# Bias attention and gated feed-forward: one queue for the loads and bias stores, and a float32 path for the first eight units

## The chip, the cores and the metric

One core of one Trainium2 chip. The metric is device time in microseconds (us) of one execution; several runs give a median, and one execution is profiled.

## What is computed

Cut to what matters (B=4, H=8, S=576, D=64; DM=512, DFF=2048):

```python
scores = q @ k.T / 8 + bias            # bias[h,i,j] = (relu(log1p(|i-j|)/log1p(max(i,1)) * w1 + b1)) @ w2
attn   = exp(scores - rowmax); attn = attn / (rowsum + 1e-9)
x      = (attn @ v) as [B*S, H*D]      # 2304 x 512
h      = x @ w_in                      # 2304 x 2048
out    = (h * sigmoid(1.702 * h)) @ w_out
```

The bias does not depend on the batch. All inputs are float32 (the weights of the feed-forward part are float64, and are loaded as pairs of 32-bit words and merged to float32).

## The kernel before, in words

**Precision.** Most products run in float16 with each operand split into a high and a low half, so one product is three float16 matmuls (high·high, high·low, low·high). The split of an operand costs a high half (a scaled copy, mostly on ACT) and a low half (`lo_part`, line 464, on DVE).

**Attention units.** There are 72 units: a query chunk c (four of 128 rows, a last one of 64), a pair of heads hp, a batch b. The first eight are all of chunk 0, batches 0 and 1. A unit runs `scores` (L601, TensorE); `reduce` (L609, DVE: adds the bias, finds the row extreme); `expo` (L618, ACT, with row sums); `inverse` (L625, L627); `exp_hi` (L639 on ACT, or L635 on DVE) and `exp_lo` (L464); `turn` (L649), a DMA transpose on SyncE's queue, which needs 16-bit data; `av` (L662, 30 float16 matmuls of 128 columns); `x_split` (L679 and L464, both on DVE), which writes the unit's part of x.

**Bias.** For each chunk c there are eight groups (four in the last chunk): four `relu` on DVE or ACT by the letters of BIAS_ENG (L382, L380), `products` (L397, float32 matmuls of 32-column weights), `bias_evict` (L400, ACT), `bias_store` (L406, a DMA to scratch memory in HBM from ACT's queue). A unit's `bias_load` (L448, SyncE's queue) waits for all stores of its chunk.

**Weights.** 32 pieces. Each is a load (L738), three merging operations on DVE (L745, L749, L753), a high half on ACT (L767), a low half on DVE (L464 into `wi` or `wo`).

**Feed-forward part.** Ten blocks of 256 rows (two of 128, blocks 4 and 9), each with 16 steps f: `m1` (L796), `tanh` (L803, ACT), `gate_mul` (L809, DVE), `gate_hi` (ACT for the blocks in ACT_G, else DVE; L817, L819), `gate_lo` (DVE for the blocks in VEC_G, else GpSimd; L824), `m2` (L833). Block 0 needs all eight first units and, by its end, all 32 weight pieces.

**Order.** Nothing is scheduled by hand. `Plan.order` is a list scheduler that runs while the kernel is built: every task has an engine, an assumed duration, dependencies, buffers taken and given back, and a priority, here a due time (`U_AT` for units, `W_AT` for weights, `B1_AT` and `B2_AT` for bias groups, leads for K, Q and V loads). The engine's instructions come out in the order the plan starts them, and each engine then executes strictly in that order: an instruction that waits holds up all behind it on its engine or queue. The plan treats at most eight DMAs of SyncE's and ACT's queues as outstanding at a time (the "hw" lanes). SLACK is added to each assumed DMA end; `hold` makes SyncE's queue busy in the plan until shortly before a transfer's assumed end.

**Queues.** Loads of q and k, 26 of the weights, V of batches 2 and 3, the bias loads and all transposes go through SyncE's queue; V of batches 0 and 1 and the first six weight pieces through GpSimd's; bias and output stores through ACT's.

```python
W_POOL = 6
(nc.gpsimd if i < W_POOL else nc.sync).dma_start(...)     # load_w
queue = nc.gpsimd if b < 2 else nc.sync                   # load_v
nc.scalar.dma_start(out=scr[c]..., in_=slot(("os", c, s))...)   # bias_store
```

Of the kernel before, what the change touches and what calls it, by code (L numbers as in the profile page):

```python
# [22 lines left out]
SLACK = 2000  # L23
# [3 lines left out]
class Plan:  # L27
# [6 lines left out]
    def add(self, eng, occ, fn, deps=(), after=(), take=(), give=(), prio=0.0, dma=0, lat=None, gate=-1, n_dma=1, mode=0, hold=False):  # L34
# [23 lines left out]
    def order(self):  # L58
# [7 lines left out]
        mode = 0  # L66
# [18 lines left out]
        while True:  # L85
            for e in ENGINES:
                while idle.get(e, 1e18) <= now and ready[e]:
# [34 lines left out]
                    if go["dma"]:  # L122
# [5 lines left out]
                        if go["hold"]:  # L128
                            occ = max(occ, end - 2000 - now)
# [34 lines left out]
def kernel(  # L164
# [45 lines left out]
    CAPS = {"ht": 6, "w64": 4, "w": 3, "kv": 3, "a32": 2, "hl": 2, "aT": 4, "bt": 3, "kT": 6, "os": 6, "qT": 3, "q": 2,  # L210
            "kt": 2, "ob": 2}
    LEAST = {"wide": {"kT": 1, "a32": 1, "hl": 1, "aT": 1, "bt": 1, "ht": 2, "w64": 1, "kv": 1},
             "narrow": {"w": 1, "os": 3, "qT": 2, "q": 1, "kt": 1, "ob": 1}}
    BIAS_ENG = ['VVVA', 'VVVA', 'VVVA', 'VVVA', 'VVVA', 'VVVA', 'VVVA', 'VVVA', 'AAAA', 'AAAA', 'AAAA', 'AAAA', 'AAAA', 'AAAA', 'VAAA', 'AAAA', 'AAAA', 'VAAA', 'AAAA', 'AAAA', 'AAAA', 'AAAA', 'AAAA', 'AAAA', 'AAAA', 'VVAA', 'VVAA', 'VVAA', 'VVAA', 'VVAA', 'VVAA', 'VVAA', 'VVVV', 'VAAA', 'VAAA', 'VVAA']
    VEC_EXP = {60: 2, 51: 1, 52: 1}
    ACT_G = {0, 3, 7}
    VEC_G = {1, 2, 7}
# [6 lines left out]
    Q_FROM, K_FROM, V_FROM = 6, 6, 4  # L224
    AV_FIRST, X_FIRST = 18.7, 6.2
# [24 lines left out]
    wi16 = cst.tile([128, 2, 4, DFF], F16, name="wi16")  # L250
    wo16 = cst.tile([128, NF, 2, DM], F16, name="wo16")
# [152 lines left out]

    def bias_store(c, s):
# [54 lines left out]
    qT_task, kT_task, v_task = {}, {}, {}  # L460
# [85 lines left out]
    def load_v(b, e):  # L546

        queue = nc.gpsimd if b < 2 else nc.sync
# [3 lines left out]
        queue.dma_start(  # L552
# [3 lines left out]
        queue.dma_start(out=t[0:64, :, 4, :], in_=va[:, SM:S, :].rearrange("u p d -> p u d"))  # L556
        queue.dma_start(
# [3 lines left out]
        queue.dma_start(  # L561
# [3 lines left out]
        queue.dma_start(out=t[64:128, :, 8, :], in_=vb[:, SM:S, :].rearrange("u p d -> p u d"))  # L565
# [370 lines left out]
```

## Time and profile before

| | |
|---|---|
| median of 3 runs | 690.97 us (690.25 to 692.12) |
| the profiled execution | 691.4 us, its span 689.6 us |
| mean granted TensorE clock | 0.954 |
| busy: PE, DVE, ACT, POOL | 617.3, 511.0, 427.8, 95.8 us (90%, 74%, 62%, 14%) |
| chain that ended last, by engine | PE 53%, DVE 21%, DMA 11%, ACT 8%, issue 4% |

PE is TensorE, DVE VectorE, ACT ScalarE, POOL GpSimd, SP SyncE; "q" behind an engine's name is its DMA queue. A busy share is an average over the span, and the stages of this kernel differ: it is read by stretches below. A row "line engine op out<-in shape xcount | busy, mean ns | idle before" is a group of equal instructions.

### The profile page before, as it was taken

The numbers are of one execution on the slowest core, as the hardware profiler recorded it, in microseconds if no ns is written. First come the engines' busy times: TensorE is split into PE (matmuls) and PEld (weight loads), VectorE is DVE, ScalarE is ACT, GpSimd is POOL, SyncE is SP. The second block draws the span as 40 slices with busy tenths as digits, with TensorE's granted clock in tenths as the row PEclk, the third lists the DMA queues.
The fourth block names the chain that finished last, engine by engine and source line by source line (L and its number), as shares of the span: only waits on it lengthen the run. The fifth ranks groups of instructions, "written<-read, shape, count | busy, mean of one in ns | idle before, by whom it ended". The sixth has DMA issues, their size and how long they took to land.

```text
span 689.6 us, 17456 instructions
## 1 busy us (share of the span) xinstructions
PE 617.3 (90%) x6888; PEld 383.7 (56%) x6888; DVE 511.0 (74%) x1432; ACT 427.8 (62%) x882; POOL 95.8 (14%) x157
## 2 busy tenths in 40 slices
PE   2766474799999998999889999999999999999997
PEld 1213242556565565656566666666666666666664
DVE  5579889999978887976877788889879884233232
ACT  2699897699967685664666766656746663222121
POOL 5210100111210000000011122111121111002222
PEclk9696875899999999999999999999999999999999
DMA  9999988998768559669998579979877763000000
GB/s 244 224 290 230 279 175 209 286 272 229 157 162 204 121 114 236 121 159 218 226 191 188 121 170 174 191 165 196 187 154 155 147 121 85 1 1 32 1 31 16
DMA packets 228082, 111.79 MB, mean 162 GB/s; under 512 B 209440, under 2 KB 211616, under 8 KB 228000
## 3 DMA queue, kind: packets, MB, share of 16 engines
q1 hardware_dynamic: 218224, 89.74, 61.4%
q10 hardware_dynamic: 7952, 15.43, 6.4%
q0 software_dynamic: 1824, 5.51, 2.6%
q8 instruction: 54, 0.88, 0.5%
q14 instruction: 28, 0.23, 0.1%
HBM read 52.85 MB, written 15.34 MB: 99 GB/s over the span
## 4 chain that ended last, share of the span: by engine, by line
PE 53%; DVE 21%; DMA 11%; ACT 8%; issue 4%; SPq 1%; POOL 0%; ACTq 0%; DVEq 0%; POOLq 0%
PE op L833 19%; PE hp L796 18%; DVE wide L464 6%; PE hp L662 6%; PE sp L601 5%; DVE wide L609 5%; DMA wide<-wide 3%; DMA wide<-in_k_dram 3%; DMA wide<-scr 2%; PE sp L397 2%; ACT wide L618 2%; ACT wide L639 2%; DVE th L809 2%; DVE narrow L749 2%; DVE narrow L753 1%
## 5 line engine op out<-in xcount | busy, mean ns | idle before, releaser
L796 PE MATMUL hp<-xT,wi 128*128 128x256 f16 (+1 forms) x1920 | 206.8, 262 | 2.6 <-DVE th L809 2.2
L833 PE MATMUL op<-wo,gT 128*128 128x512 f16 x864 | 205.2, 380 | 0.9 <-POOL gT L824 0.6
L796 PEld LDWEIGHTS <-wi 128*128 128x128 f16 x1920 | 170.3, 98 | 39.1 <-issue 10.4
L618 ACT ACTIVATE wide<-wide,sm 128x576 f32<-128x576 f32 x144 | 110.6, 769 | 93.1 <-DVE sm L609 92.7
L824 POOL TENSOR_TENSOR gT<-th,gT 128x256 f16<-128x256 f32 (+1 forms) x112 | 76.1, 681 | 536.3 <-ACT gT L817 302.0
L833 PEld LDWEIGHTS <-gT 128*128 128x128 f16 x864 | 77.8, 98 | 91.3 <-issue 5.5
L464 DVE SCALAR_TENSOR_TENSOR wide<-wide,sm,wide 128x576 f16<-128x576 f32 x144 | 119.4, 843 | 12.3 <-ACT wide L639 11.9
L803 ACT ACTIVATE th<-hp 128x256 f32<-128x256 f32 (+1 forms) x160 | 56.7, 355 | 100.6 <-PE hp L796 91.0
L809 DVE SCALAR_TENSOR_TENSOR th<-th,hp 128x256 f32<-128x256 f32 (+1 forms) x160 | 62.3, 390 | 72.4 <-ACT th L803 71.7
L609 DVE CUSTOM_DVE_ANT_0 wide<-sp,wide 128x576 f32<-128x576 f32 x144 | 105.3, 750 | 10.9 <-DMA wide<-scr 5.4
L639 ACT ACTIVATE wide<-wide,sm 128x576 f16<-128x576 f32 x140 | 103.8, 766 | 5.5 <-issue 3.0
L601 PE MATMUL sp<-wide,narrow 64*128 64x512 f16 (+1 forms) x960 | 69.5, 295 | 16.7 <-DVE wide L464 7.5
L662 PEld LDWEIGHTS <-v 128*64 128x64 f16 x2400 | 67.4, 114 | 26.6 <-issue 23.2
L662 PE MATMUL hp<-wide,v 128*64 128x128 f16 (+1 forms) x2190 | 67.1, 215 | 4.9 <-DMA wide<-wide 4.8
L380 ACT ACTIVATE wide<-tab,bp 128x576 f32<-128x576 f32 x96 | 69.3, 767 | 2.8 <-ACT narrow L400 1.6
L601 PEld LDWEIGHTS <-narrow 64*128 64x128 f16 (+1 forms) x960 | 29.5, 99 | 50.4 <-issue 30.1
L397 PE MATMUL op<-wide,pk 128*32 128x512 f32 (+1 forms) x224 | 34.1, 546 | 11.8 <-ACT wide L380 5.7
L625 DVE TENSOR_SCALAR sm<-sm 128x1 f32<-128x1 f32 x144 | 21.5, 149 | 21.2 <-ACT wide L618 20.4
L819 DVE CAST gT<-th 128x256 f16<-128x256 f32 (+1 forms) x112 | 30.8, 275 | 6.4 <-PE op L833 0.2
L397 PE MATMUL sp<-wide,pk 128*32 128x512 f32 (+1 forms) x352 | 29.4, 456 | 2.2 <-DVE sm L609 1.9
L397 PEld LDWEIGHTS op<-wide,pk 128*32 128x32 f32 x224 | 10.3, 130 | 35.2 <-ACT wide L380 14.4
L679 DVE TENSOR_SCALAR xT<-hp 128x128 f16<-128x128 f32 x72 | 20.4, 283 | 12.2 <-PE hp L662 11.9
(63 smaller groups left out, 451.5 us busy)
## 6 DMA issues: line engine op xcount, KB each, us to landing
wide<-scr SPq DMA_DIRECT2D x32, 576.0 KB, 5.3
scr<-narrow ACTq DMA_DIRECT2D x33, 288.0 KB, 3.5
wide<-in_moe_w_out_dram SPq DMA_DIRECT2D x14, 512.0 KB, 5.1
wide<-in_moe_w_in_dram SPq DMA_DIRECT2D x12, 512.0 KB, 5.5
wide<-in_k_dram SPq DMA_DIRECT2D x16, 256.0 KB, 5.3
narrow<-in_q_dram SPq DMA_DIRECT2D x16, 256.0 KB, 5.0
out_dram<-narrow ACTq DMA_DIRECT2D x16, 256.0 KB, 3.4
wide<-scr SPq DMA_DIRECT2D x8, 288.0 KB, 5.2
```

The source lines that it names most:

```text
L380: nc.scalar.activation(out=h, in_=tv, func=ACTF.Relu, bias=bp[:, pb:pb + 1])
L397: nc.tensor.matmul(to[32 * r:32 * r + 32], lhsT=w2b, rhs=rhs, start=True, stop=True)
L464: nc.vector.scalar_tensor_tensor(out=out, in0=in0, scalar=scale, in1=in1, op0=ALU.mult, op1=ALU.subtract)
L601: nc.tensor.matmul(pair[64 * e:64 * e + m, a, cs], lhsT=qt[r, x, hp + e, 0:m], rhs=kt[r, hp % 2 + e, y, cs], start=i == 0, stop=i == 2,)
L609: nc.vector.tensor_tensor_reduce(out=slot(("a32", u))[:, cs], in0=slot(("sp", u)).rearrange("p (h a) n -> p h (a n)", h=2)[:, a, 0:S], in1 ...
L618: nc.scalar.activation(out=t, in_=t, func=ACTF.Exp, scale=-1.0, bias=sm[:, a:a + 1], accum_out=sm[:, 2 + a:3 + a])
L639: nc.scalar.activation(out=hl_of(u)[:, 0, cs], in_=slot(("a32", u))[:, cs], func=ACTF.Identity, scale=r)
L662: nc.tensor.matmul(o[64 * a:64 * a + 64, po], lhsT=vt[:, x, vc:vc + 64], rhs=t[:, 9 * y + k0, po], start=kb < 0 and i == 0, stop=kb == 3 a ...
L796: nc.tensor.matmul(p[:, :n], lhsT=wi16[:, z, cc, 128 * f:128 * f + 128], rhs=r, start=i == 0, stop=i == 11,)
L809: nc.vector.scalar_tensor_tensor(out=th, in0=th, scalar=1.0, in1=slot(("hp", j, f))[:, :n], op0=ALU.add, op1=ALU.mult)
L824: (nc.vector if j in VEC_G else nc.gpsimd).tensor_tensor(out=gt[:, 1, :n], in0=th, in1=gt[:, 0, :n], op=ALU.subtract)
L833: nc.tensor.matmul(o[:, i], lhsT=gt[:, z, ts], rhs=wo16[:, f, y, :], start=f == 0 and n3 == 0, stop=f == NF - 1 and n3 == 2,)
```

## The change

All loads and the bias stores are issued on SyncE's queue. The first eight units (DIRECT = 8) no longer split their exponentials: DVE builds a diagonal matrix of the reciprocal row sums, TensorE multiplies the float32 exponentials by it, which transposes and scales them into PSUM, ACT or DVE copies that to SBUF, and `av_direct` multiplies in float32 with the unsplit values V. For these units `exp_hi`, `exp_lo`, the DMA transpose and the float16 `av` are gone. Beside this the first half of `x_split` goes to ACT for 11 units, 52 `exp_hi` are put on DVE outside the first eight units (4 before), 65 `relu` are on DVE (48 before; by chunk 24, 1, 7, 24, 9 where it was 24, 1, 1, 14, 8), blocks 0, 2, 3, 5, 6, 8, 9 have `gate_hi` on ACT (0, 3, 7 before), blocks 4 to 7 `gate_lo` on DVE (1, 2, 7 before), and the due times, leads, SLACK and buffer limits change. The weight buffers are laid out anew (`wi16`, `wo16` in one tile). A second way to hand over the first bias chunk (`bias_place`, `bias_keep`) is written down but PLACE is False, so it is not built.

```diff
-SLACK = 2000
+SLACK = 3000
...
-                            occ = max(occ, end - 2000 - now)
+                            occ = max(occ, end - go["hold"] - now)
...
-    CAPS = {"ht": 6, "w64": 4, "w": 3, "kv": 3, "a32": 2, "hl": 2, "aT": 4, "bt": 3, "kT": 6, "os": 6, "qT": 3, "q": 2,
+    CAPS = {"ht": 6, "w64": 4, "w": 3, "kv": 6, "a32": 3, "hl": 2, "aT": 4, "bt": 3, "kT": 6, "os": 6, "qT": 3, "q": 2, "dg": 2,
...
-    U_AT = (41.8, 8, 104.8, 8.89)
-    W_POOL = 6
-    W_AT = (19.7, 3, 5, 51.6, 1.95)
-    B1_AT = (10.5, 4.18)
-    B2_AT = (10.3, 6)
-    BT_LEAD, K_LEAD, Q_LEAD, V_LEAD, LOAD_LEAD, W_LEAD = -0.4, 5, 5, 6.5, 12, 12.2
+    DIRECT = 8
+    TURN_OUT = ['AAV', 'AAV', 'VAA', 'VAA', 'AAV', 'VAA', 'VVV', 'VVA']
+    X_ACT = {1, 2, 4, 6, 7, 8, 10, 12, 13, 14, 15}
+    V_LATE = {(0, 0): -21.9, (1, 0): 18.2, (0, 1): 138.3, (1, 1): 123.3}
+    U_AT = (17.5, 9.67, 92.1, 8.12)
+    W_FREE = 5
+    PLACE = False
+    W_AT = (1.0, 6.75, 9, 50.7, 5.81)
+    B1_AT = (6.1, 3.56)
+    B2_AT = (-6.7, 8.24)
+    BT_LEAD, K_LEAD, Q_LEAD, V_LEAD, LOAD_LEAD, W_LEAD = -5.9, 16.7, -4.2, 43.9, 4.3, -7.7
...
     def bias_store(c, s):
-        nc.scalar.dma_start(
+        nc.sync.dma_start(
...
-            scr_done[c].append(add("ACT", 20, lambda c=c, s=s: bias_store(c, s), [ev], give=[("os", c, s)],
+            scr_done[c].append(add("SP", 350, lambda c=c, s=s: bias_store(c, s), [ev], give=[("os", c, s)],
...
-        queue = nc.gpsimd if b < 2 else nc.sync
-        queue.dma_start(
+        nc.sync.dma_start(
...
+    def diagonal(u, a):
+        nc.vector.tensor_scalar(
+            out=slot(("dg", u))[:, 128 * a:128 * a + 128], in0=idn, scalar1=small[u % 8][:, 2 + a:3 + a], scalar2=None,
+            op0=ALU.mult,
+        )
+
+    def turn_pe(u, a):
+        t, d = slot(("a32", u)), slot(("dg", u))[:, 128 * a:128 * a + 128]
+        o, h = slot(("pt", u))[:, a], slot(("pt2", u))
+        nc.tensor.matmul(
+            h[64 * a:64 * a + 64, 0:128], lhsT=t[:, 512 + 64 * a:576 + 64 * a], rhs=d, start=True, stop=True,
+        )
+        for kb in range(4):
+            x = 640 * a + 128 * kb
+            nc.tensor.matmul(o[:, 128 * kb:128 * kb + 128], lhsT=t[:, x:x + 128], rhs=d, start=True, stop=True)
+
+    def turn_out(u, a):
+        t = slot(("aT", u))[:, 640 * a:640 * a + 512]
+        if TURN_OUT[u][a] == "A":
+            nc.scalar.copy(t, slot(("pt", u))[:, a])
+        else:
+            nc.vector.tensor_copy(t, slot(("pt", u))[:, a])
...
+        for kb in range(-1, 4):
+            for a in range(2):
+                po = slice(64 * a, 64 * a + 64) if kb < 0 else slice(0, 128)
+                k0 = 4 if kb < 0 else 5 * a + kb
+                nc.tensor.matmul(
+                    o[64 * a:64 * a + 64, 0:128], lhsT=vd[po, k0], rhs=t[po, k0],
+                    start=kb < 0, stop=kb == 3, skip_group_check=True,
+                )
...
+        if z == 0 and u in X_ACT:
+            nc.scalar.activation(out=d[:, 0], in_=o[:, 0:128], func=ACTF.Copy, scale=xs)
...
-        (nc.gpsimd if i < W_POOL else nc.sync).dma_start(out=slot(("w64", i))[:, 0:1024].bitcast(U32), in_=src)
+        nc.sync.dma_start(out=slot(("w64", i))[:, 0:1024].bitcast(U32), in_=src)
```

`turn_tail`, not shown, copies the last 64 key columns of both heads (128 x 128) from PSUM.

## Rows read from the trace of the kernel before

**Rows 1.** Busy time by stretch; columns: stretch, its length, five engines, clock, DMA, GB/s.

```profile
0.00:60.00 60.00, 32.38 (x232) 12.53 (x232) 38.60 (x87) 39.58 (x66) 16.45 (x40) 0.83 0.89 252
60.00:140.00 80.00, 52.80 (x575) 29.80 (x579) 74.12 (x183) 66.25 (x122) 5.84 (x8) 0.74 0.95 239
140.00:200.00 60.00, 58.90 (x640) 35.35 (x633) 55.62 (x138) 54.72 (x108) 10.90 (x13) 1.00 0.85 214
200.00:600.00 400.00, 388.75 (x4784) 248.82 (x4783) 316.62 (x948) 248.05 (x537) 45.02 (x64) 1.00 0.76 158
650.00:690.00 40.00, 34.48 (x322) 23.33 (x320) 11.88 (x42) 7.87 (x24) 10.82 (x22) 0.97 0.07 21
```

**Rows 2.** The chain that ended last, 0 to 130 us: start, length, what.

```profile
2.67 15.60 DMA wide<-in_k_dram
...
36.27 6.67 DMA scr<-narrow
43.21 7.71 DMA wide<-scr
```

**Rows 3.** DVE's groups by line and form, 0 to 60 us, with idle time before them.

```profile
L464 DVE SCALAR_TENSOR_TENSOR wide<-sp,wide 128x1152 f16<-128x1152 f32 x2 | 2.7, 1358 | 5.9 <-ACT wide L536 5.9
L357 DVE COPY ips<-hp 128x36 f32<-128x36 f32 x1 | 0.2, 196 | 6.7 <-ACT tab L339 6.7
```

**Rows 4.** DVE's groups by line and form, 0 to 200 us.

```profile
L464 DVE SCALAR_TENSOR_TENSOR wide<-wide,sm,wide 128x576 f16<-128x576 f32 x32 | 26.1, 825 | 0.0
...
L753 DVE SCALAR_TENSOR_TENSOR narrow<-wide,narrow 128x512 uint32<-128x512 uint32 x32 | 22.7, 711 | 0.1
L749 DVE SCALAR_TENSOR_TENSOR narrow<-wide,narrow 128x512 uint32<-128x512 uint32 x32 | 22.0, 687 | 0.1
L382 DVE TENSOR_SCALAR wide<-tab,bp 128x576 f32<-128x576 f32 x30 | 14.1, 525 | 1.7 <-PE op L397 1.6
L745 DVE TENSOR_SCALAR narrow<-wide 128x512 uint32<-128x512 uint32 x32 | 13.7, 429 | 0.0
L464 DVE SCALAR_TENSOR_TENSOR wi<-narrow,wi 128x512 f16<-128x512 f32 x16 | 11.0, 687 | 1.0 <-ACT wi L767 0.9
L464 DVE SCALAR_TENSOR_TENSOR wo<-narrow,wo 128x512 f16<-128x512 f32 x16 | 10.9, 684 | 3.6 <-ACT wo L767 3.5
L809 DVE SCALAR_TENSOR_TENSOR th<-th,hp 128x256 f32<-128x256 f32 x16 | 6.6, 414 | 0.7 <-ACT th L803 0.7
...
L679 DVE TENSOR_SCALAR xT<-hp 128x128 f16<-128x128 f32 x16 | 4.5, 282 | 3.0 <-PE hp L662 3.0
```

**Rows 5.** DVE's and ACT's groups by line and form, whole span.

```profile
L639 ACT ACTIVATE wide<-wide,sm 128x576 f16<-128x576 f32 x140 | 103.8, 766 | 5.5 <-issue 3.0 <-DVE sm L627 1.8 <-ACT wi L767 0.2
...
L819 DVE CAST gT<-th 128x256 f16<-128x256 f32 x80 | 23.1, 289 | 3.9 <-PE op L833 0.2
...
L635 DVE TENSOR_SCALAR wide<-wide,sm 128x576 f16<-128x576 f32 x4 | 2.0, 512 | 0.0
```

**Rows 6.** PE in order of time: start, length, instructions in a run.

```profile
16.21 1.08 PE L524 MATMUL sp<-idn,wide 128*128 128x128 f32 x4 [4.54 <-DMA wide<-in_k_dram]
...
88.59 1.81 PE L662 MATMUL hp<-wo,v 128*64 128x128 f16 x30
...
96.02 0.66 PE L524 MATMUL sp<-idn,wide 128*128 128x128 f32 x4 [0.28 <-DVE sm L609]
```

**Rows 7.** PE's groups by form, 84.7 to 86.3 us, clock low.

```profile
L601 PE MATMUL sp<-wide,narrow 64*128 64x512 f16 x6 | 1.6, 606 | 6.0 <-DVE wide L464 6.0
L397 PE MATMUL op<-wide,pk 128*32 128x512 f32 x2 | 1.1, 1060 | 0.0
```

**Rows 8.** DMA issues 30 to 60 us: queue, count, KB each, us from issue to landing.

```profile
wide<-scr SPq DMA_DIRECT2D x3, 576.0 KB, 10.1
scr<-narrow ACTq DMA_DIRECT2D x4, 288.0 KB, 5.4
...
wide<-in_moe_w_in_dram SPq DMA_DIRECT2D x2, 512.0 KB, 11.6
```

More of the change, by code (lines that the diff above doesn't have):

```diff
@@ L32, in __init__, with add @@
         self.env, self.refs = {}, {}
-    def add(self, eng, occ, fn, deps=(), after=(), take=(), give=(), prio=0.0, dma=0, lat=None, gate=-1, n_dma=1, mode=0, hold=False):
+    def add(self, eng, occ, fn, deps=(), after=(), take=(), give=(), prio=0.0, dma=0, lat=None, gate=-1, n_dma=1, mode=0, hold=0):
         t = dict(eng=eng, occ=occ, fn=fn, deps=list(deps), after=list(after), take=list(take), give=[], prio=prio,
@@ L410 @@
     t_near = [t_sd, t_sa, t_iv]
+    placed = []
     t_far = None
@@ L451 @@
         bk = (c, hp, b // 2)
-        if bk not in bt_task:
+        if (u >= 8 or not PLACE) and bk not in bt_task:
             bt_key[bk] = ("bt", u)
@@ L643, in exp_lo, with turn_tail, av_direct @@
         lo_part(hl_of(u)[:, 1, cs], slot(("a32", u))[:, cs], r, hl_of(u)[:, 0, cs])
+    def diagonal(u, a):
[18 more added lines that the diff above has]
+            nc.vector.tensor_copy(t, slot(("pt", u))[:, a])
+    def turn_tail(u):
+        t, o = slot(("aT", u))[:, 512:640], slot(("pt2", u))[:, 0:128]
+        nc.scalar.copy(t, o) if TURN_OUT[u][2] == "A" else nc.vector.tensor_copy(t, o)
+    def av_direct(u):
+        b, c, hp = units[u]
+        t = slot(("aT", u)).rearrange("p (c n) -> p c n", c=9)
+        o = slot(("ot", u))
+        vd = slot(("v32", b, hp // 2)).rearrange("p (u c d) -> p u c d", u=2, c=9)[:, hp % 2]
+        for kb in range(-1, 4):
[5 more added lines that the diff above has]
+                    start=kb < 0, stop=kb == 3, skip_group_check=True,
+                )
     def aT_of(u):
@@ L705 @@
         for a in range(2):
-            t = add("DVE", 676, lambda u=u, a=a: reduce(u, a), [st, bt_task[bk]],
+            t = add("DVE", 676, lambda u=u, a=a: reduce(u, a), [st] + (placed if PLACE and u < 8 else [bt_task[bk]]),
                     take=[("wide", "a32", ("a32", u))] if a == 0 else [], after=[t] if a else [],
-                    give=([("sp", u)] + ([bt_key[bk]])) if a else [], prio=p + 0.1 + 0.01 * a, lat=160)
+                    give=([("sp", u)] + ([] if PLACE and u < 8 else [bt_key[bk]])) if a else [], prio=p + 0.1 + 0.01 * a, lat=160)
+            if PLACE and u < 8:
+                first_use.append(t)
             ex = add("ACT", 757, lambda u=u, a=a: expo(u, a), [t], prio=p + 0.2 + 0.01 * a)
@@ L712 @@
                 iv = add("DVE", 65, lambda u=u, a=a, part=part: inverse(u, a, part), [iv], prio=p - 900)
+            if u < DIRECT:
+                dg = add("DVE", dve(128, ptr=1, fast=True), lambda u=u, a=a: diagonal(u, a), [iv], prio=p - 800,
+                         take=[("narrow", "dg", ("dg", u))])
+                tp = add("PE", 1200, lambda u=u, a=a: turn_pe(u, a), [dg], mode=4, prio=p - AV_FIRST - 1,
+                         take=[("o", "pt", ("pt", u)), ("h", "pt2", ("pt2", u))] if a == 0 else [],
+                         after=[tp] if a else [], give=[("dg", u), ("a32", u)])
+                los.append(add("ACT" if TURN_OUT[u][a] == "A" else "DVE", act(512, True) if TURN_OUT[u][a] == "A" else dve(512),
+                               lambda u=u, a=a: turn_out(u, a), [tp], take=[("wide", "aT", ("aT", u))],
+                               give=[("pt", u)], prio=p - 5))
+                if a:
+                    los.append(add("ACT" if TURN_OUT[u][2] == "A" else "DVE", act(128, True) if TURN_OUT[u][2] == "A" else dve(128),
+                                   lambda u=u: turn_tail(u), [tp], give=[("pt2", u)], prio=p - 5))
+                continue
             ev = a < VEC_EXP.get(u, 0)
```

99 lines of the change are left out of this document (63 added, 36 removed).

## The prediction

> **What bounds the kernel now.** I read the busy time by stretch first [rows 1]. From 200 to 600 us TensorE works 388.75 of 400 us at granted clock 1.00: it is the bound there, and only 11.25 us are left in its gaps. DVE is busy 317 of those 400 us and ACT 248. In the last 40 us TensorE is idle for 5.5 us. Before 200 us it is otherwise: TensorE is busy 32.4 of 60 us, then 52.8 of 80 at a mean clock of 0.74. DVE is busy 74.1 of 80 us from 60 to 140 and 55.6 of 60 from 140 to 200. So the kernel has a beginning that DVE sets and a long rest that TensorE sets. The reader is to see that a busy share over the span (DVE 74%) hides this.
>
> Which work marks the end of the beginning? By 200 us DVE has done 16 first halves of x (16 units), 16 `gate_mul` (all steps of block 0) and all 32 weight pieces [rows 4]. I call this the **milestone**. Every later block finds the weights ready, so if the milestone comes earlier by some time and the rest is unchanged, the end comes earlier by that time. DVE's account up to it is 38.6 + 74.1 + 55.6 = 168.3 us of work and 31.7 us of idle time [rows 1]. The weights alone are 22.7 + 22.0 + 13.7 + 11.0 + 10.9 = 80.3 us of that [rows 4].
>
> Of the idle time 21.4 us lie before 60 us. The chain there [rows 2] goes through K's load, 15.6 us, then through the last store of the first bias chunk, 6.67 us, and its load back, 7.71 us, so that the first unit's reduction cannot begin before 51 us. DVE's own waits agree: 6.7 us until the first tables have come, 5.9 us for ACT's half of K [rows 3].
>
> **The change part by part, by DVE's account to the milestone.**
>
> *Float32 path.* Removed: 16 `exp_lo` at 0.825 us, -13.2 [rows 4]. Added: 16 diagonals, 128x128 from SBUF with one scalar per row. None is in the trace; the ends are 0.11 us (0.512 us for 576 columns of L635, [rows 5], by columns alone) and 0.28 us (L679, same size but from PSUM, [rows 4]); I take 0.2, between them because a short operation has a fixed part: +3.2. Seven copies of 128x512 out of PSUM by the letters of TURN_OUT, with 0.43 us (L745) and 0.69 us (L464 into `wi`) as ends [rows 4]; I take the upper, since the source is PSUM: +4.8. Four tails at L679's 0.28: +1.1. Sum -4.1, ends -7.3 to -2.8.
>
> *Moved halves.* 11 first halves of x go to ACT, 11 x 0.282 = -3.1; six more `relu` of chunk 2 come to DVE, 6 x 0.525 = +3.2 [rows 4]. Sum 0. ACT, busy 39.6 + 66.3 + 54.7 = 160.5 of 200 us [rows 1], loses 16 x 0.766 = 12.3 us of `exp_hi` [rows 5] and gets nine copies, four tails and the 11 halves, about 24 operations of 0.3 to 0.7 us: roughly even.
>
> *Loads on one queue.* GpSimd issued the first six weight pieces and V of batches 0 and 1; they shared the DMA engines with K, whose 15.6 us stand first in the chain. In the new order tables, K and the first weights follow each other on one queue by due time, V of heads 4 to 7 is split late, and no weight load stands behind a waiting transpose of the first eight units. I expect DVE's wait of 5.9 us for K to go, and of the 8.8 us left before 60 us (21.4 - 6.7 - 5.9) about 3 to be filled with weight pieces that are there earlier. Of the 10.3 us of idle time from 60 to 200 us I take 2 off. Sum -11. Ends: -20 (all but the first 6.7 us and 5 us of the rest) and +4 (the stores, below).
>
> *Stores on the same queue.* 36 stores change queue. In the full stretch a store by ACT's queue landed after 5.4 us, loads on SyncE's after 10.1 and 11.6 us [rows 8]. The nearest row for a store behind loads is the load's, so the last store of chunk 0 may take 10.1 instead of 6.67 us, +3.4; against this the loads ahead of it are fewer by then. Behind a store that waits for its `bias_evict` stand the next loads and transposes; whoever waits for those waits too. I take +0 for the sum, as the earlier K moves the whole bias chain forward, and keep +4 as the end. GpSimd is freed, which nobody waits for, and ACT's store issues vanish from its stream, which I cost at nothing because ACT is not the bound. The Trainium skill ("DMA: Bandwidth & Descriptors", Queues, rings and completion order) says that each DMA engine takes turns between the queues that have work; by that a store on its own queue passes loads that it must follow on a shared one. Rows 8 point the same way, 5.4 against 10.1 us, and no run here has shown a store on SyncE's queue.
>
> *TensorE.* Per unit 10 transposing and 10 multiplying float32 matmuls of 128 columns come, 30 float16 ones go (1.81 us at the low clock, [rows 6]). The trace has no full-width float32 multiplication. The float32 transposes of L524 take 0.27 us each at the low clock (1.08 / 4) and 0.165 at the high one [rows 6]. Lower end 0.165; upper end 1.06, a float32 matmul of 512 columns [rows 7], which should be too much by about four. That points to 0.27 as well, and I take it: 20 x 0.27 - 1.81 = 3.6 us per unit, 29 us for eight. TensorE is idle for 27.2 us from 60 to 140 us [rows 1], and more work should lift the clock, which was 0.74. So it is just covered: +0. Without that cover it costs its surplus (a rival). What is late next is then `turn_out` and the reductions on DVE.
>
> *The rest.* After 200 us DVE gets 48 more `exp_hi` at 0.512 (+24.6), 11 `relu` (+5.8) and some 4 us of `gate_lo`; three more blocks' worth of `gate_hi` leave it (48 casts of 0.289, -13.9, and 16 narrower ones) [rows 4, 5]. Net about +17 on 317 of 400 us: TensorE still covers it. Sum 0, ends -5 (half of the gaps) and +6. The tail stays.
>
> **Sum:** -4 + 0 - 11 + 0 + 0 + 0 = -15 us against the profiled execution's 691.4 us, which is 0.4 us above the median of the runs: 676.4, so **676 us**. The ends of the terms give 691 - 7 - 20 - 5 = 659 to 691 - 3 + 4 + 6 = 698, without the upper end of the float32 price, which is rival 1's.
>
> **The rivals.**
> 1. *TensorE becomes the bound of the first eight units* (slower). At 0.45 us per float32 matmul the extra work is (20 x 0.45 - 1.81) x 8 = 57.5 us against 27.2 us of idle time, 30 us too much: 676 + 30 = **706**. It eats the whole gain from (27 + 15) / 8 = 5.25, (5.25 + 1.81) / 20 = 0.35 us per matmul. For it: L397's float32 columns cost 1060 ns where float16 ones cost 606 [rows 7], and the chain scores, reduce, exponential, diagonal, transpose, copy, multiply runs twice through TensorE's fixed order. Against it: the transposes at 0.165 us, and the clock of 1.00 wherever TensorE is busy [rows 1, 6]. Chance 0.13. The Trainium skill ("FP8 and Floating Point Precision", TensorE Precision Notes) says that true float32 needs four passes through the array, which by columns alone would be an estimate of 0.43 us at the low and 0.21 at the high clock, so rival 1 at the low clock and my forecast at the high one.
> 2. *One queue, no gain*: stores that wait hold up the loads, the first reduction stays at 51 us or comes 4 us later, and the -11 are lost: 691.4 - 4 + 4 = **691**. For it: [rows 8]; SyncE's queue then carries loads, transposes and stores in a fixed order. Against: K's load, the first link, has nothing of this ahead of it. Chance 0.14, a third of it slower.
> 3. *A larger gain*: the idle time goes down to 12 us (-20), TensorE's gaps after 200 us halve (-5) with the longer SLACK: 691.4 - 4 - 20 - 5 = **662**. For it: the due times of the weights are stretched, so DVE has units to do when a piece is missing. Chance 0.15.
> 4. *It isn't what it says*: the placing of the first bias in SBUF is not built (PLACE is False), so the way through scratch memory stays. This is certain and is in the sum.
>
> **How the numbers follow.** The forecast (668 to 686) has 0.53, rival 3 0.15, rival 1 0.13, rival 2 0.14, and 0.05 goes to steady-state losses on the fuller DVE. About 0.3%, 2.1 us, is what a measurement can tell from no change. Faster: 0.53 + 0.15 and a quarter of rival 2, 0.71. Slower: rival 1, a third of rival 2 and part of the rest, 0.20. Same: 0.09. The range, leaving out the top of rival 1 and the bottom of rival 3, is 658 to 697.
>
> **What would show it.** In the profile after: the first reduction (the line of L609) at about 41 us instead of 51; DVE's idle time before 200 us about 20 instead of 32; the milestone at about 185 us; TensorE busier and at a higher clock from 60 to 140 us; float32 matmuls of `turn_pe` and `av_direct` at 0.17 to 0.3 us apart; gaps after 200 us near 11 us. I am wrong if the first reduction isn't earlier, if DVE waits for PSUM filled by TensorE between 50 and 130 us (rival 1), or if the milestone moves but gaps after 200 us take it back.

## The result, and the profile after

| | before | after |
|---|---|---|
| median of the runs made together | 691.55 us (690.25 to 692.14, 4 runs) | 673.94 us (672.60 to 676.46, 4 runs) |
| profiled execution, its span | 691.4, 689.6 us | 672.78, 671.0 us |
| mean granted TensorE clock | 0.954 | 0.990 |

The ratio is 0.9766, 95% interval 0.9735 to 0.9798: 17.6 us less. The forecast was 676 us. Medians here and below are over executions of the ordinary speed; one of e5's ten took 1276.79 us and is left out.

First comes the busy time by stretch after the change, with the columns of [rows 1]; the second fence is the same view of the kernel before, cut at the milestone instead of at 200 us. The milestone (the last of 16 units' x, 32 weight pieces, 16 `gate_mul` of block 0) ends at 188.9 us after and at 198.2 us before.

```profile
0.00:60.00 60.00, 41.94 (x372) 20.53 (x374) 46.80 (x106) 47.54 (x78) 3.62 (x19) 0.97 0.93 271
60.00:140.00 80.00, 63.56 (x634) 41.41 (x630) 73.36 (x193) 61.38 (x130) 3.85 (x5) 0.96 0.71 204
...
0.00:188.90 188.90, 153.22 (x1530) 91.00 (x1534) 168.01 (x412) 151.50 (x295) 17.04 (x35) 0.97 0.80 224
200.00:600.00 400.00, 395.49 (x4824) 256.06 (x4817) 329.57 (x977) 222.56 (x509) 35.17 (x45) 1.00 0.74 154
```

```profile
0.00:198.20 198.20, 142.29 (x1424) 76.11 (x1425) 167.28 (x402) 158.74 (x292) 33.20 (x61) 0.85 0.91 237
```

Three things are to be seen. DVE's work to the milestone did not fall: 168.0 us after, 167.3 before. Its idle time did, from 198.2 - 167.3 = 30.9 to 188.9 - 168.0 = 20.9 us. And after 200 us the gaps of TensorE shrank from 11.25 us [rows 1] to 400 - 395.49 = 4.5 us. In spans: 689.6 - 671.0 = 18.6 us, of which 9.3 are the milestone and 9.3 what follows it (491.4 to 482.1 us). TensorE's whole busy time is 617.3 us before and 625.6 after, so after the milestone it works 475.0 and 472.4 us: of the second 9.3 us, 6.7 are idle time (16.4 to 9.7) and 2.6 work, part of which now stands before the milestone (24 more records of `m1`, L890).

Where did DVE's saving go? Its groups by line and form, 0 to 200 us, after:

```profile
L842 DVE SCALAR_TENSOR_TENSOR narrow<-wide,narrow 128x512 uint32<-128x512 uint32 x32 | 23.7, 742 | 0.4
...
L846 DVE SCALAR_TENSOR_TENSOR narrow<-wide,narrow 128x512 uint32<-128x512 uint32 x32 | 22.2, 693 | 0.3
L389 DVE TENSOR_SCALAR wide<-tab,bp 128x576 f32<-128x576 f32 x42 | 19.9, 516 | 0.1
L487 DVE SCALAR_TENSOR_TENSOR wide<-wide,sm,wide 128x576 f16<-128x576 f32 x19 | 15.4, 831 | 0.8 <-ACT wide L664 0.8
...
L487 DVE SCALAR_TENSOR_TENSOR wide<-sp,wide 128x1152 f16<-128x1152 f32 x4 | 5.4, 1350 | 1.3 <-ACT wide L559 1.3
...
L691 DVE COPY wide<-op 128x512 f32<-128x512 f32 x7 | 4.8, 686 | 3.3 <-PE op L684 1.3 <-ACT wide L643 1.0 <-ACT v L595 1.0
...
L671 DVE TENSOR_SCALAR narrow<-idn,sm 128x128 f32<-128x128 f32 x16 | 4.1, 279 | 0.2
```

`exp_lo` (L487 from `wide` to `wide`) fell from 32 to 19 [rows 4], but `relu` (L389) rose from 30 to 42, 38 of them ahead of the milestone (+3.8 us), and the three merges take 742, 693 and 451 ns where they took 687, 711 and 429 (L749, L753, L745 of rows 4): 1.9 us more for 32 pieces. DVE's wait for ACT's half of K is 1.3 us where it was 5.9 [rows 3].

The first reduction begins at 39.83 us; it began at 51.06 (DVE in order of time, after and then before):

```profile
38.62 1.29 DVE L487 SCALAR_TENSOR_TENSOR v<-wide,v 128x512 f16<-128x512 f32 x2 [0.36 <-ACT v L595]
39.83 0.75 DVE L634 CUSTOM_DVE_ANT_0 wide<-sp,wide 128x576 f32<-128x576 f32 x1
```

```profile
51.06 0.76 DVE L609 CUSTOM_DVE_ANT_0 wide<-sp,wide 128x576 f32<-128x576 f32 x1 [1.38 <-DMA wide<-scr]
```

The chain that ended last, 0 to 130 us, after, no longer goes through a load of K, a store or a load back ahead of it (the columns are those of [rows 2]):

```profile
0.75 5.21 DMA pk<-in_pack_dram
...
11.37 1.05 PE sp L547 x4
13.55 1.13 ACT wide L559
16.03 1.29 PE op L404 x16
...
25.61 2.10 ACT wide L387 x3
...
32.59 2.81 PE op L404 x15
...
39.11 2.22 ACT wide L387 x4
41.69 1.61 ACT wide L643 x4
...
80.21 3.09 DMA wide<-in_v_dram
```

Behind it DVE, ACT and TensorE take turns, with one load of V among them. These are the float32 matmuls, PE in order of time after, first at clock 1.00, then in a stretch at the lower of the two levels (clock 0.50, and 0.54 for the last row):

```profile
45.06 0.43 PE L679 MATMUL hp<-narrow,wide 128*64 128x128 f32 x2
45.43 1.16 PE L684 MATMUL op<-narrow,wide 128*128 128x128 f32 x8
...
48.40 1.46 PE L706 MATMUL hp<-wide,wide 64*64 64x128 f32 x20 [0.38 <-DVE wide L695]
...
102.24 2.60 PE L706 MATMUL hp<-wide,wide 64*64 64x128 f32 x20 [3.30 <-DVE wide L695]
...
106.50 2.00 PE L684 MATMUL op<-narrow,wide 128*128 128x128 f32 x8
```

Each float32 matmul stands as two records: four transposing ones (L684) are 8 records in 1.16 us, 0.29 us each, and 0.50 each in the last row; ten multiplying ones (L706) are 20 records in 1.46 us, and 2.60 at the low level. Over all eight units, PE's groups of the whole span after:

```profile
L684 PE MATMUL op<-narrow,wide 128*128 128x128 f32 x128 | 19.4, 297 | 0.1
...
L706 PE MATMUL hp<-wide,wide 128*64 128x128 f32 x128 | 10.1, 298 | 0.4 <-DVE wide L691 0.4
...
L679 PE MATMUL hp<-narrow,wide 128*64 128x128 f32 x32 | 6.8, 296 | 6.4 <-ACT narrow L407 3.2 <-DVE narrow L671 2.0 <-DVE sm L652 1.2
L706 PE MATMUL hp<-wide,wide 64*64 64x128 f32 x32 | 3.7, 313 | 3.7 <-DVE wide L695 3.7
```

That is 40.0 us, 5.0 per unit, so 25.5 us more than the 8 x 1.81 of float16 that went [rows 6].

### The profile page after: what moved, and what is told of

Read it like the earlier page. It is cut to its first block, busy times and chain, and to the rows that moved or that the text cites. A ratio compares the mean times of both kernels' runs of the same rounds, so it can differ in the third digit from the quotient of the medians.

```text
span 671.0 us, 17480 instructions
## 1 busy us (share of the span) xinstructions
PE 625.6 (93%) x6968; PEld 397.4 (59%) x6968; DVE 519.3 (77%) x1449; ACT 405.8 (60%) x889; POOL 72.2 (11%) x115
## 4 chain that ended last, share of the span: by engine, by line
PE 61%; DVE 23%; ACT 8%; DMA 3%; issue 3%; SPq 0%; ACTq 0%; DVEq 0%
PE op L927 22%; PE hp L890 22%; PE hp L728 6%; PE sp L625 5%; DVE wide L634 4%; DVE wide L487 4%; PE sp L404 2%; ACT wide L643 2%; DVE narrow L842 2%; ACT wide L387 2%; DVE w L487 2%; DVE narrow L846 2%; PE op L404 2%; DVE th L903 2%; DMA wide<-wide 1%
## 5 line engine op out<-in xcount | busy, mean ns | idle before, releaser
L890 PE MATMUL hp<-xT,w 128*128 128x256 f16 (+1 forms) x1920 | 208.4, 262 | 3.1 <-DVE th L903 1.0
L927 PE MATMUL op<-w,gT 128*128 128x512 f16 x864 | 204.7, 380 | 0.6 <-POOL gT L918 0.2
L890 PEld LDWEIGHTS <-w 128*128 128x128 f16 x1920 | 170.5, 98 | 40.9 <-issue 10.6
L487 DVE SCALAR_TENSOR_TENSOR wide<-wide,sm,wide 128x576 f16<-128x576 f32 x128 | 104.9, 829 | 7.0 <-ACT wide L664 6.6
L625 PE MATMUL sp<-wide,narrow 64*128 64x512 f16 (+2 forms) x960 | 66.3, 286 | 6.0 <-DVE sm L634 3.0
L911 ACT CAST gT<-th 128x256 f16<-128x256 f32 (+1 forms) x112 | 43.2, 386 | 36.1 <-DVE th L903 35.7
L664 ACT ACTIVATE wide<-wide,sm 128x576 f16<-128x576 f32 x76 | 57.8, 768 | 9.2 <-DVE sm L652 5.0
L387 ACT ACTIVATE wide<-tab,bp 128x576 f32<-128x576 f32 x79 | 58.0, 768 | 1.2 <-DVE tab L351 1.2
L404 PE MATMUL op<-wide,pk 128*32 128x512 f32 (+1 forms) x224 | 25.4, 471 | 11.2 <-ACT wide L689 3.2
L389 DVE TENSOR_SCALAR wide<-tab,bp 128x576 f32<-128x576 f32 x65 | 32.6, 534 | 0.1
L660 DVE TENSOR_SCALAR wide<-wide,sm 128x576 f16<-128x576 f32 x52 | 27.2, 523 | 1.4 <-PE sp L404 0.9
```

The source lines that it names most:

```text
L387: nc.scalar.activation(out=h, in_=tv, func=ACTF.Relu, bias=bp[:, pb:pb + 1])
L404: nc.tensor.matmul(to[32 * r:32 * r + 32], lhsT=w2b, rhs=rhs, start=True, stop=True)
L487: nc.vector.scalar_tensor_tensor(out=out, in0=in0, scalar=scale, in1=in1, op0=ALU.mult, op1=ALU.subtract)
L625: nc.tensor.matmul(pair[64 * e:64 * e + m, a, cs], lhsT=qt[r, x, hp + e, 0:m], rhs=kt[r, hp % 2 + e, y, cs], start=i == 0, stop=i == 2,)
L664: nc.scalar.activation(out=hl_of(u)[:, 0, cs], in_=slot(("a32", u))[:, cs], func=ACTF.Identity, scale=r)
L890: nc.tensor.matmul(p[:, :n], lhsT=wi16[:, f // 4, cc, z, 128 * (f % 4):128 * (f % 4) + 128], rhs=r, start=i == 0, stop=i == 11,)
```

## The experiments

Twelve kernels ran. Some change one operation and leave every other instruction where it was ("order kept"); the others change an input of the planner, which then lays out everything anew ("planned anew"). This table, worked out from the profiles (us), is used throughout. Rest is the span less the milestone; idle is the stretch less the busy time.

| kernel | median | milestone | rest | DVE work, idle to milestone | TensorE idle to milestone, after it |
|---|---|---|---|---|---|
| before | 691.55 | 198.2 | 491.4 | 167.3, 30.9 | 55.9, 16.4 |
| after | 673.94 | 188.9 | 482.1 | 168.0, 20.9 | 35.7, 9.7 |
| **order kept** | | | | | |
| e3 stores on ACT's queue | 674.46 | 190.9 | 483.1 | 167.8, 23.1 | 36.1, 10.6 |
| e4 V, weights on GpSimd's queue | 675.41 | 191.5 | 482.2 | 168.3, 23.2 | 36.5, 9.7 |
| e5 transposing matmuls twice | 687.00 | 204.4 | 482.1 | 168.4, 36.0 | 34.4, 9.7 |
| e6 reductions twice | 686.34 | 202.4 | 482.2 | 180.1, 22.3 | 42.0, 9.9 |
| e12 one merge left out | 664.71 | 182.2 | 482.2 | 148.8, 33.4 | 30.5, 9.4 |
| **planned anew** | | | | | |
| e1 due times 0.3 later | 676.42 | 191.2 | 483.0 | 168.8, 22.4 | 38.4, 10.2 |
| e2 no float32 path | 690.33 | 199.7 | 491.0 | 177.6, 22.1 | 58.4, 14.3 |
| e7 old division of work | 675.65 | 185.6 | 487.7 | 167.2, 18.4 | 33.8, 14.5 |
| e8 old due times | 697.72 | 208.4 | 489.3 | 172.2, 36.2 | 45.3, 15.4 |
| e9 shorter merge | 679.20 | 192.2 | 485.6 | 147.5, 44.7 | 35.0, 11.2 |
| e10 e9 with PLACE | 673.95 | 188.1 | 484.2 | 146.8, 41.3 | 37.3, 10.6 |
| e11 SLACK 2000 | 683.74 | 195.5 | 488.3 | 167.9, 27.6 | 38.7, 13.4 |

The table answers one question at once: with the order kept the rest stays at 482.1 to 483.1 us whatever happens before it, so the milestone sets the end, one for one, as the prediction assumed.

**How much does a new plan move by itself?** e1 shifts two due times by a third of a microsecond:

```diff
-    U_AT = (17.5, 9.67, 92.1, 8.12)
+    U_AT = (17.8, 9.67, 92.4, 8.12)
```

> The changed kernel with the units' due times 0.3 us later throughout and nothing else. No theory gives this a cause to be faster or slower; it measures how much the end depends on the accidents of the plan's order. Expected 674 us, within 3 us; if it moves by more, differences of that size between variants whose order was planned anew mean nothing.

Measured: 676.42 us, ratio to before 0.9797 (0.9768 to 0.9826). A change that means nothing costs 2.5 us here (2.3 at the milestone, 0.9 in the rest); of kernels planned anew, differences of that size are not read. One such shift is a single sample: others may move the time by more.

**The stores' queue.** e3 puts the bias stores back on ACT's queue, in the same places of the order:

```diff
     def bias_store(c, s):
-        nc.sync.dma_start(
+        nc.scalar.dma_start(
```

> The changed kernel with the bias stores issued from ACT's queue again, at the same places of the unchanged order. Theory A (which queue the stores use costs nothing, since ACT is not the bound and stores land early either way): 674 us, within 2 us. Rival C (a store on SyncE's queue waits behind loads and holds loads back): faster, 670 us or less. Rival D (stores on ACT's queue hold ACT up, and their removal is part of the gain): slower, 678 us or more.

Measured: 674.46 us, ratio 0.9764 (0.9734 to 0.9794). No difference. From 30 to 60 us the four stores landed after 5.0 us on ACT's queue and 4.3 on SyncE's (DMA issues of the two kernels; in after the row is):

```profile
scr<-narrow SPq DMA_DIRECT2D x4, 288.0 KB, 4.3
```

The bound of +4 us from [rows 8] (10.1 us for a load on SyncE's queue) did not apply. The stretch moves as many bytes after as before (276 and 278 GB/s), yet the loads from scratch memory land after 5.3 us on the same queue; before, a DMA transpose was among its transfers, after not. Whether that is the reason was not tried. The Trainium skill ("DMA: Bandwidth & Descriptors", Queues, rings and completion order) has each DMA engine take turns between queues; by that the shared queue should have been the slower one, and these two runs show no such cost.

**The loads' queue.** e4 puts V of batches 0 and 1 and the first six weight pieces back on GpSimd's queue, order kept:

```diff
-        nc.sync.dma_start(out=slot(("w64", i))[:, 0:1024].bitcast(U32), in_=src)
+        (nc.gpsimd if i < 6 else nc.sync).dma_start(out=slot(("w64", i))[:, 0:1024].bitcast(U32), in_=src)
```

> The changed kernel with V of batches 0 and 1 and the first six weight pieces loaded by GpSimd's queue again, at the same places of the unchanged order. Theory A (K came late before because six weight loads ran beside it on another queue): the first K transposition goes back from 11.4 toward 16 us, and the first reduction from 39.8 toward 45 us or later; 678 to 684 us. Rival E (the order of the plan alone moved K forward, and the queue doesn't matter): first K transposition at 11 to 12 us and 674 us within 2 us.

Measured: 675.41 us, ratio 0.9771 (0.9741 to 0.9802). PE in order of time still has K's first transposition at the same place:

```profile
11.42 1.11 PE L547 MATMUL sp<-idn,wide 128*128 128x128 f32 x4
```

It was 16.21 before [rows 6], and the first reduction of e4 starts at 40.00 us. So with the order of the plan kept, it does not matter which queue these loads use: the shared queue is not what brought the start forward.

**The float32 path alone missing.** e2 keeps the new due times, division and queues and plans the first eight units the old way:

```diff
-    DIRECT = 8
+    DIRECT = 0
-ps_ = V_LATE[b, e] if b < 2 else p
+ps_ = p
```

> The changed kernel with the float32 path switched off (DIRECT = 0, V's halves split by the same rule as for batches 2 and 3), planned anew. Theory A (the milestone is set by DVE, and most of the gain is the earlier first chain and filled idle time): the path gives back DVE's 4 us and the eight transposes' places on SyncE's queue, so 678 to 682 us, about a third of the gain lost. Rival B (the float32 path is the gain, by TensorE's higher clock and the missing transposes): 688 to 692 us.

Measured: 690.33 us, ratio 0.9994 (0.9972 to 1.0015). Busy by stretch:

```profile
60.00:140.00 80.00, 43.95 (x499) 24.18 (x493) 72.83 (x178) 61.36 (x117) 0.00 (x0) 0.68 0.97 244
```

The first reduction begins at 38.92 us, as early as after, yet the eighth unit's x ends at 134.1 instead of 115.3 us (128.8 before): the start's gain is lost between 40 and 134 us, where TensorE works 43.95 of 80 us at clock 0.68. But DVE is nearly full there. Busy time up to the eighth x, e2 first, then after:

```profile
38.00:134.00 96.00, 54.65 (x560) 27.74 (x560) 87.66 (x216) 79.06 (x146) 0.00 (x0) 0.68 0.97 249
```

```profile
38.00:115.30 77.30, 57.77 (x553) 38.51 (x551) 68.58 (x184) 59.30 (x119) 0.00 (x0) 0.96 0.68 212
```

DVE does 87.66 us of work where it does 68.58 after, 19.1 us more, as much as the eighth x is late (18.8). TensorE's longest waits in that stretch are for DVE's reductions (12.9 and 7.4 us in all), and its list of waits there names no DMA transpose. Up to the milestone e2 keeps what the earlier start gives (DVE is idle 22.1 us, 8.8 less than before) and spends it on 10.3 us more DVE work; against after it has 9.6 us more work and 1.2 us more idle time. So what the path saves may be DVE's work as well as TensorE's time at a low clock, and no run separates the two. One confound stays: five `exp_hi` of these units go to DVE in this kernel, 5 x 0.51 us.

**The new due times alone missing.** e8 takes U_AT, W_AT, B1_AT, B2_AT, the leads and five neighbouring numbers from before, and keeps the rest:

```diff
-    U_AT = (17.5, 9.67, 92.1, 8.12)
+    U_AT = (41.8, 8, 104.8, 8.89)
...
-    W_AT = (1.0, 6.75, 9, 50.7, 5.81)
+    W_AT = (19.7, 3, 5, 51.6, 1.95)
...
```

> The changed kernel with all due times, leads and gates of before, planned anew. Theory A (the due times put K first, ask for weights early and then stretch them): the first reduction goes from 39.8 us to 45 us or later, the milestone from 189 to 195 us or later, 680 to 688 us. Rival B (the float32 path carries the gain whatever the due times): 673 to 677 us.

Measured: 697.72 us, ratio 1.0107 (1.0071 to 1.0144): slower than before, and above both expected ranges. The last weight piece ends at 174.6 us, 14 us earlier than after, but the sixteenth x at 208.4 instead of 186.1. So either half, taken back alone, takes the whole gain away. The float32 path takes 16 us off with the new due times; with the old ones the kernel is slower than before, and the new due times without the path gain nothing. (After, e2 and e8 share the new division of work, SLACK, queues and buffer limits; the old kernel with only the path or only the due times was not run.) K's first transposition and the first reduction of e8:

```profile
16.18 0.66 PE L547 MATMUL sp<-idn,wide 128*128 128x128 f32 x4
```

```profile
42.92 0.75 DVE L634 CUSTOM_DVE_ANT_0 wide<-sp,wide 128x576 f32<-128x576 f32 x1
```

The transposition is as late as before, but by its place in the order: TensorE's wait of 4.54 us for K's load [rows 6] and DVE's of 5.9 us for ACT's half of K [rows 3] are gone here too. The first reduction is 3.1 us later than after, of the 11.2 us by which the change brought it forward. Which part of the change brings the other 8.1 us stays open; the buffer limits (CAPS) and the times that K's and Q's loads hold the queue in the plan changed as well, and no run takes them back.

**Is there cover on TensorE?** e5 issues `turn_pe`'s matmuls twice, order kept:

```diff
-        for kb in range(4):
+        for kb in [0, 1, 2, 3] * 2:
```

(the tail's matmul likewise).

> The changed kernel with every float32 transposing matmul of the first eight units issued twice, the order unchanged: 80 more matmuls at 0.145 us (8 took 1.16 us) is 11.6 us and the tails add about 5, so some 16 us more work on TensorE between 43 and 112 us, where it is idle for about 18 us. Theory A (TensorE has cover there, DVE sets the pace): the milestone moves by 0 to 5 us, 674 to 679 us. Rival F (TensorE's fixed order is on the chain of the first units): nearly all of it shows, 686 to 690 us.

Measured: 687.00 us, ratio 0.9961 (0.9945 to 0.9977), 13.1 us more than after. PE's groups by form, 0 to 140 us, which hold all eight units:

```profile
L685 PE MATMUL op<-narrow,wide 128*128 128x128 f32 x256 | 32.8, 281 | 0.0
L680 PE MATMUL hp<-narrow,wide 128*64 128x128 f32 x64 | 10.1, 280 | 7.6 <-ACT narrow L407 3.1 <-ACT w L861 1.3 <-DVE narrow L671 1.2
```

Both passes take 42.9 us where one took 19.4 + 6.8 = 26.2: the second adds only 16.7, while the mean clock up to the milestone rose from 0.97 to 1.00, so that the first pass became shorter too. (The expectation had 0.145 us per matmul, which is the time per record, half of a matmul; its 16 us came out by luck.) TensorE was idle 35.7 us before the milestone, and 34.4 us still are: of 16.8 us of added busy time 1.3 found cover, and the span grew by 15.5; by the medians (13.1 us) it would be 3.7. Idle time on TensorE is not free room here: its stream is in a fixed order, and in its idle time it waits for DVE or ACT (the last columns of the rows above).

**Is there cover on DVE?** e6 does the same to DVE: each reduction of the first eight units twice, 16 x 0.75 = 12 us, order kept.

```diff
+        for _ in range(2 if u < DIRECT else 1):
             nc.vector.tensor_tensor_reduce(
```

> The changed kernel with the reduction of the first eight units run twice (the second writes the same values), the order unchanged: 16 x 0.75 = 12 us more work on DVE, as much as the path's removal of exp_lo took away. Theory A (DVE sets the beginning): milestone 8 to 13 us later, 682 to 687 us. Rival B (the float32 path gains through TensorE's clock and the missing transposes): DVE has 21 us of idle time before the milestone, so 674 to 677 us.

Measured: 686.34 us, ratio 0.9937 (0.9917 to 0.9958), 12.4 us more than after for 12.1 us more work, one for one. DVE's idle time did not take up any of it (20.9 to 22.3).

**And does taking work away gain as much?** e12 leaves the second merging operation of all 32 pieces out, order kept, so the weights lack the lowest 3 of float32's 23 fraction bits:

```diff
         elif part == 1:
-            nc.vector.scalar_tensor_tensor(
-                out=w, in0=lo, scalar=29, in1=w, op0=ALU.logical_shift_right, op1=ALU.bitwise_or
-            )
+            pass
```

> The second merging operation of each of the 32 weight pieces is left out of the instructions, so the low bits of the weights are missing (work left out); the plan and so the order of every other instruction stay as in the kernel after. DVE has 32 x 0.693 = 22.2 us less work before the milestone. Theory A (DVE's stream is the beginning, one for one in both directions, as 12 us of added reductions cost 12.4 us): about 652 us, milestone near 167 us. Theory M (the beginning is a chain that passes through TensorE, DVE and ACT in a fixed order, so work added to either engine shows, but work taken from DVE only turns into waits for the next loads, exponentials and turned tiles): 664 to 672 us, milestone later than 178 us, DVE's idle time before it above 28 us. Theory F (TensorE alone sets the beginning): no change, 672 to 675 us.

Measured: 664.71 us, ratio 0.9628 (0.9590 to 0.9666), 9.2 us less than after in the medians and 6.6 in the spans. DVE has 19.3 us less work up to the milestone and 12.5 us more idle time. The waits say where it went; DVE's waits up to the milestone, first after, then e12 (waited for, us, times, longest):

```profile
DVE ips L364 <- ACT tab L346: 6.6, 1, 6.6
DVE w L487 <- ACT w L860: 4.5, 5, 1.6
DVE sm L650 <- ACT wide L643: 1.5, 2, 1.3
DVE wide L691 <- PE op L684: 1.3, 1, 1.3
```

```profile
DVE w L487 <- ACT w L858: 8.9, 9, 1.9
DVE ips L364 <- ACT tab L346: 6.6, 1, 6.6
DVE wide L691 <- PE op L684: 3.7, 3, 2.2
DVE sm L650 <- ACT wide L643: 2.5, 5, 1.3
DVE th L901 <- ACT th L895: 1.9, 6, 0.6
```

The same waits grew, on ACT's half of the weights and on the turned tile from TensorE. Work added to either of the two links tested here, TensorE and DVE, shows nearly in full; work taken from one of them shows by a third to a half (6.7 us at the milestone or 9.2 in the medians, of 19.3), and the other links take the rest.

**The same saving, planned anew.** In e9 the planner knows that the merge is shorter; e10 also sets PLACE, so that the first bias chunk stays in SBUF. Both leave out the same operation as e12.

```diff
-        for part in range(3):
+        for part in (0, 2):
```

> The changed kernel without the second of the three merging operations of each weight piece (the lowest three bits of a float32 weight are left at zero; the halves written to wi and wo keep fewer bits than that), planned anew. It takes 32 x 0.69 = 22 us of DVE's work away from the beginning. Theory A (DVE's work sets the beginning, and time on it shows one for one as the doubled reduction did): milestone 12 to 20 us earlier, 656 to 663 us. Rival F (the first units' chain through all engines sets it, and DVE's weight work only fills holes): milestone 0 to 6 us earlier, 668 to 675 us.

> As the one before, and with PLACE true: the first bias chunk is put into SBUF and the first eight units read it there, without the way through scratch memory. Theory A: the first reduction comes some 4 to 8 us before 39.8 us (no load back of 5 us), but DVE has weight work to fill that wait already, so 0 to 4 us on top: 653 to 663 us. Rival F (the chain that begins with the first reduction sets the milestone): all of it on top of whatever the shorter merge gives, 4 to 8 us less than the run before.

Measured: 679.20 us, ratio 0.9854 (0.9831 to 0.9877), and 673.95 us, ratio 0.9781 (0.9761 to 0.9800), e9 above both of its expected ranges. The output of e9 is off by some 3%; e10 and e12 leave out the same bits without that, so something else goes wrong somewhere in e9's order, and its time is not read. (For the same reason the 5.3 us from e9 to e10 don't speak for rival F, and the earlier first reduction that was to bring them did not come.) In e10 the planner's new order loses what e12 gains with the old one: DVE is idle 41.3 us, and with PLACE the first reduction comes 3.7 us later than after, where 4 to 8 us earlier were expected:

```profile
43.52 0.76 DVE L634 CUSTOM_DVE_ANT_0 wide<-sp,w 128x576 f32<-128x576 f32 x1 [4.84 <-DMA wide<-in_v_dram]
```

That the due times fit only the durations for which they were chosen is a guess: they were not chosen anew for the shorter merge.

**What closed the gaps after 200 us?** e7 takes back the division of work (BIAS_ENG, VEC_EXP, ACT_G, VEC_G, X_ACT), e11 the longer SLACK:

```diff
...
-    X_ACT = {1, 2, 4, 6, 7, 8, 10, 12, 13, 14, 15}
+    X_ACT = set()
...
-    ACT_G = {0, 2, 3, 5, 6, 8, 9}
+    ACT_G = {0, 3, 7}
...
```

> The changed kernel with the division of work between ACT, DVE and GpSimd as before the change (BIAS_ENG, VEC_EXP, ACT_G, VEC_G as before, all first halves of x on DVE), planned anew. Theory G (the new division closed TensorE's gaps after 200 us, 11.25 us before and 4.5 after): gaps back to 9 us or more, 678 to 682 us. Rival H (the longer SLACK or the due times closed them): gaps stay at 4 to 6 us, 673 to 677 us.

```diff
-SLACK = 3000
+SLACK = 2000
```

> The changed kernel with SLACK 2000 as before the change, planned anew. Theory G (the new division of work closed the gaps after 200 us): gaps stay at 4 to 6 us, 673 to 677 us. Rival H (SLACK closed the waits for transposes): PE's wait for transposes in av after 200 us goes from 0.5 us back to 3 to 5 us and the gaps to 8 us or more, 677 to 681 us.

Measured: e7 675.65 us, ratio 0.9795 (0.9762 to 0.9829); e11 683.74 us, ratio 0.9915 (0.9879 to 0.9950). From 200 to 600 us the gaps are 9.1 and 8.4 us (400 less PE busy), against 4.5 after and 5.0 in e1; e7 first, then e11:

```profile
200.00:600.00 400.00, 390.93 (x4784) 251.69 (x4782) 311.43 (x938) 247.19 (x535) 45.14 (x64) 1.00 0.73 155
```

```profile
200.00:600.00 400.00, 391.57 (x4780) 250.92 (x4779) 328.48 (x976) 222.29 (x513) 34.66 (x46) 1.00 0.79 158
```

The rest is 5.6 us longer in e7 and 6.2 in e11 than after (0.9 in e1). e7 has the milestone 3.3 us earlier, little more than what e1's shift does, so in all the new division is worth less than a new plan's accidents. e11 loses another 6.6 us ahead of the milestone, which nobody expected: it is above both expected ranges, and SLACK is not a matter of the gaps alone. Nor does it work through the transposes alone: TensorE waits for transposed exponentials 1.3 us in e11, where it waited 4.8 us before and 0.5 after (PE's waits, 200 to 600 us, before, after, e11):

```profile
PE hp L662 <- DMA wide<-wide: 4.8, 4, 2.3
```

```profile
PE hp L728 <- DMA wide<-wide: 0.5, 1, 0.5
```

```profile
PE hp L728 <- DMA wide<-wide: 1.3, 2, 0.8
```

e2 and e8 wait 4.1 and 5.5 us for them although they keep the long SLACK, and they have wide gaps too (9.4 and 14.2 us, e8's in part ahead of its milestone) with the new division and SLACK. So each of these parts, taken back alone, brings back more than half of the 6.7 us of idle time. They don't add up to shares, and which single wait closes them stays open.

## Why the prediction was right, and where its steps were not

The time (676 for 673.94) and the side were right, and so was the frame: a beginning up to a milestone, then a full TensorE. Constant rests with the order kept bear it out. The milestone was forecast at about 185 us and came at 188.9; the first reduction at 41, and came at 39.83; the mean clock from 60 to 140 us was to rise from 0.74, and came to 0.96. The gaps after 200 us were to stay near 11 us, and shrank to 4.5.

- *Float32 path, DVE -4.1.* The parts came nearly as priced: the copies 686 ns for 0.69 us, the tails 280 for 0.28. The diagonals took 279 ns, the upper end, where 0.2 was taken; in all 4.1 us of busy time for 3.2. With 13.5 us of `exp_lo` gone (26.1 to 12.6) the path's own sum is -3.5. But DVE's work to the milestone rose by 0.7. What failed is the account around the path: the new order puts eight more `relu` ahead of the milestone, where six were counted, the merges are 1.9 us slower over 32 pieces, and the rest is spread over small groups.
- *Loads on one queue, -11.* The size was nearly right: idle time fell by 10.0 us, and K's wait went from 5.9 to 1.3. The cause was not the queue: e4 gives the loads their old queues and keeps 40.00 us for the first reduction. The due times account for 3.1 of the 11.2 us (e8), and DVE's wait for K is as short in e4 (1.4 us) and gone in e8; what else moved the start is open. And the early start alone is worth nothing (e2).
- *Stores, +0.* Right (e3). The upper end of +4 had no ground in these runs.
- *TensorE just covered, +0.* The size was close, 25.5 us for 29, but by luck. The price of 0.27 us was that of a float32 transposition at the low clock, which stands as one record. The matmuls that came, two records each, took 0.29 (transposing) and 0.15 us (multiplying) at the high clock, 0.50 and 0.26 near the low one. All at the low level they would have come to (10 x 0.50 + 10 x 0.26 - 1.81) x 8 = 46 us, an estimate from these rows, far above the idle time that was to cover them; most ran at the high one (clock 0.97 to the milestone), and the multiplying kind was cheap there. The Trainium skill ("FP8 and Floating Point Precision", TensorE Precision Notes) has four passes for true float32, by columns alone an estimate of 0.21 us at the high clock; the trace has 0.29 and 0.15. The reason given, idle time that swallows the work, is not borne out: e5 finds 1.3 us of cover in 35.7 (3.7 by the medians) for a second pass, and for the first no run measures it. What can be seen is that the path replaces waiting: without it (e2) TensorE is idle 58.4 us up to the milestone at clock 0.84, and DVE has 9.6 us more to do; with it TensorE is idle 35.7 us at 0.97. Rival 1 did not come true, but e5 shows its mechanism near: a second pass brings 13.1 us.
- *The rest, 0 (-5 to +6).* The step that failed most: idle time after the milestone fell by 6.7 us and the work by 2.6, 9.3 together, beyond the end. Rival 3 had this (gaps halved by SLACK, -5). Taking SLACK back (e11) brings back 3.7 of the 6.7 us, but the old division (e7) brings back 4.8, so SLACK is not the cause by itself.

So a milestone gain of 9.3 for 15 and a rest of -9.3 for 0 made up for each other: that the total came so near is luck. Rival 2's condition (first reduction not earlier) did not occur, and rival 4 was as said.

Of the versions run, e12 is the fastest, 664.71 us, for whoever can do without the weights' three lowest bits.

## What to carry to other kernels

Idle time on an engine whose instructions stand in a fixed order need not be cover, since what it waits for may be on the same chain: double one operation with the order kept and see. Added work may show nearly in full where removed work shows by a third to a half. When a change moves a planner's inputs and the operations together, taking back either part may lose the whole gain; and before a small difference between two plans is read, run one with a meaningless shift (2.5 us here). Fix a milestone and check that the rest stays constant: then a time before it can be read one for one.

## What was not expected of the hardware

A float32 matmul stands in the trace as two records (L684: 128 for 64), a float32 transposition as one (L547: 64 for 64), so a time per record is not a time per matmul. The full-width transposing ones (128 x 128 weights, 128 columns) took 0.29 us each at granted clock 1.00, while ten multiplying ones with 64-column weights took 1.46 us, half as much each. With 16 turns' worth of matmuls added (e5) the mean clock to the milestone rose from 0.97 to 1.00, and one pass fell from 26.2 us to about 21.5 (half of 42.9); adding DVE work (e6) lowered it to 0.93, and the same transposing group took 25.4 us instead of 19.4:

```profile
L685 PE MATMUL op<-narrow,wide 128*128 128x128 f32 x128 | 25.4, 360 | 0.0
```

So more DVE work, with TensorE waiting longer for it (idle 42.0 us to the milestone for 35.7), also made TensorE's own work slower, which was not priced in the prediction.
